# Halves and two PSUM banks at the start of a four-layer kernel, a bias transpose moved into K, a weight load moved ahead, and two layernorm statistics moved to ScalarE

## Chip, cores, metric

One core of one Trainium2 chip. The metric is the device time of one execution in microseconds (us), over several executions. Beside it stands the *span* in this text: the time from the first to the last of the program's own instructions in the profile, which every timed run reports too.

## The reference

```python
x = A_x                                             # (1, 2048, 1024) bf16
x = x + A(layernorm(x), wqkv, wo)                   # attention: 32 heads of 32, each position looks at
x = x + B(layernorm(x), w1, b1, w2, b2)             #   8 positions, 2 apart; B: 1024 -> 3584, gelu, -> 1024
x = x + A(layernorm(x), wqkv, wo)
x = x + B(layernorm(x), w1, b1, w2, b2)
```

## The kernel before

The 2048 rows are worked on in four groups of 512 rows (four tiles of 128). TensorE does Q, K, V, the output projection (with the weights Wq, Wk, Wv and Wo) and the two feed-forward products for one group after the other, in one fixed order. It puts its results into PSUM tiles, here one bank each, and VectorE or ScalarE copies them out. VectorE does the attention of one group while TensorE is at the products of another. The argument needs the start of the program and the first group's Q and K. `vec`, `act`, `pool` and `sp` are VectorE, ScalarE, GpSimd and the engine that issues most DMAs; with `.on` an engine keeps the order of the program text.

```python
load_x(0, 0, 2)                                     # x tiles 0 and 1
for k in range(0, KD, 2):                           # four pieces of Wq, 512 KB each, with x tiles 2 and 3 between
    load_wq_piece(...)
...
def ln_first():
    ...
    stats(0)                                        # VectorE: bn_stats x2, bn_aggr; ScalarE: sqrt
    stats(1)
    xn0 = norm(0)                                   # VectorE: reciprocal, (x - mean) * rstd
    xn1 = norm(1)
    transpose_on_pe(xn0, xa[0][:, 0, :, :], parts=[act.copy] * 4)      # 8 transposes into one PSUM bank, then copies
    ps = transpose_bias()                                              # b1, 28 x 128, on TensorE
    transpose_on_pe(xn1, xa[0][:, 1, :, :], parts=[vec.tensor_copy] * 2 + [act.copy] * 2)
    warm_up(2)                                                         # two matmuls of zeros
    act.copy(b1T[:], ps[:])
    stats(2); stats(3); ...
...
# first group: Q of tiles 0 and 1 as soon as they are there, then tiles 2 and 3, K, V
wk = load_qkv(1)
early_tiles = ln_early((1, None), (2, qk_next))     # groups 1 and 2: statistics and norm on VectorE, DMA transposes
...
# the main program
warm_up(14)
ln_first()
build_constants()
load_x(1)
load_x(2)                                           # third x group, ahead of Wk
stage(gen_qkv(0, qk_next=early), sides=at(14, load_b2))
```

## Time and profile before

| | kernel before |
|---|---|
| time, first three runs | 1230.68 us (1230.61 to 1230.74) |
| span of the profiled run | 1229.1 us |
| TensorE busy | 99% of the span |
| first useful matmul | 8.95 us |
| pitch of the 512-wide matmuls, 138 us to the end | 215.8 ns, no holes |

In the groups of instructions and in the timelines, a line has the start and the length in us, the engine, the source line (a helper's, as a rule), the operation, and out<-in by the program's names; brackets hold the idle time of the engine ahead of it and what ended it. PE is TensorE's matmuls, PEld its weight loads, SPq the queue that issues DMAs. The end of a matmul is modelled, so starts are what to reckon with. The lines that the argument rests on are in the prediction.

### The profile page before, as it was taken

The numbers are of one execution on the slowest core, as the hardware profiler recorded it, in microseconds if no ns is written. First come the engines' busy times: TensorE is split into PE (matmuls) and PEld (weight loads), VectorE is DVE, ScalarE is ACT, GpSimd is POOL, SyncE is SP. The second block draws the span as 40 slices with busy tenths as digits, with TensorE's granted clock in tenths as the row PEclk, the third lists the DMA queues.
The fourth block names the chain that finished last, engine by engine and source line by source line (L and its number), as shares of the span: only waits on it lengthen the run. The fifth ranks groups of instructions, "written<-read, shape, count | busy, mean of one in ns | idle before, by whom it ended". The sixth has DMA issues, their size and how long they took to land.

```text
span 1229.1 us, 13953 instructions
## 1 busy us (share of the span) xinstructions
PE 1221.3 (99%) x5723; PEld 632.7 (51%) x5773; DVE 864.2 (70%) x918; ACT 315.1 (26%) x507; POOL 105.2 (9%) x209
## 2 busy tenths in 40 slices
PE   9999999999999999999999999999999999999998
PEld 7666544456444564446544465444654444444444
DVE  8999896998997999375993759937599797011001
ACT  4343253014410144202441024410244001400310
POOL 3010015010101101100001000010000002000000
PEclk9999999999999999999999999999999999999999
DMA  9954674756648745856557565576664558446441
GB/s 299 293 205 154 178 238 153 201 171 206 215 133 239 188 151 167 235 169 181 155 160 233 171 171 175 155 222 202 171 199 145 189 195 203 155 160 195 154 136 52
DMA packets 220031, 226.64 MB, mean 184 GB/s; under 512 B 68194, under 2 KB 187136, under 8 KB 217920
## 3 DMA queue, kind: packets, MB, share of 16 engines
q1 hardware_dynamic: 214704, 208.69, 56.9%
q0 software_dynamic: 5264, 17.06, 3.6%
q8 instruction: 45, 0.74, 0.2%
q14 instruction: 18, 0.15, 0.0%
HBM read 189.01 MB, written 4.19 MB: 157 GB/s over the span
## 4 chain that ended last, share of the span: by engine, by line
PE 99%; DVE 0%; issue 0%; DMA 0%
PE acc L117 99%; DMA x<-in_A_x_dram 0%; DVE stats L92 0%; PE acc L218 0%; DVE xn L92 0%; DVE x L92 0%; DVE mv L92 0%; PE acc L181 0%; DVE rstd L92 0%
## 5 line engine op out<-in xcount | busy, mean ns | idle before, releaser
L117 PE MATMUL acc<-xnT,wt 128*128 128x512 bf16 (+1 forms) x3392 | 720.3, 375 | 0.1
L117 PEld LDWEIGHTS <-wt 128*128 128x128 bf16 x3392 | 400.8, 119 | 318.0 <-issue 0.5
L117 PE MATMUL acc<-wt,hT 128*128 128x512 bf16 (+1 forms) x1780 | 386.0, 376 | 2.1
L117 PEld LDWEIGHTS <-hT 128*128 128x128 bf16 x1820 | 178.1, 98 | 209.0
L92 DVE TENSOR_TENSOR big<-big 128x1024 bf16<-128x1024 bf16 (+2 forms) x184 | 244.7, 1358 | 2.2
L92 ACT ACTIVATE hT<-acc,b1T 128x512 bf16<-128x512 f32 x224 | 152.1, 687 | 325.1 <-PE acc L117 325.0
L92 DVE TENSOR_TENSOR big<-qT,kT 128x4096 bf16<-128x4096 bf16 x64 | 143.8, 2284 | 36.4 <-ACT kT L92 35.9
L92 DVE TENSOR_TENSOR tmp<-acc,b2bc 128x512 f32<-128x512 f32 x56 | 38.6, 689 | 161.6 <-PE acc L117 158.5
L92 DVE TENSOR_TENSOR big<-abc,vT 128x4096 bf16<-128x4096 bf16 x64 | 144.6, 2284 | 9.8 <-DMA abc<-a 7.4
L92 ACT CAST qT<-acc 128x512 bf16<-128x512 f32 (+1 forms) x72 | 38.2, 543 | 277.6 <-PE acc L117 277.6
L117 PE MATMUL acc<-wt,oT 128*128 128x512 bf16 x440 | 97.6, 379 | 0.5
L92 DVE BATCH_NORM_STATS2 stats<-x 128x6 f32<-128x512 bf16 x120 | 79.9, 680 | 3.7 <-DMA x<-in_A_x_dram 2.7
L117 PEld LDWEIGHTS <-oT 128*128 128x128 bf16 x448 | 43.8, 98 | 53.0 <-DVE oT L92 0.3
L92 DVE TENSOR_TENSOR x<-acc,big 128x512 bf16<-128x512 f32 (+1 forms) x9 | 5.7, 632 | 90.1 <-PE acc L117 90.0
L92 ACT CAST vT<-acc 128x512 bf16<-128x512 f32 x64 | 37.4, 585 | 100.9 <-PE acc L117 100.8
L92 POOL TENSOR_TENSOR rstd<-mv,eps_t 128x1 f32<-128x1 f32 x56 | 17.4, 311 | 527.5 <-DVE mv L92 527.5
L92 ACT CAST kT<-acc 128x512 bf16<-128x512 f32 x64 | 37.3, 585 | 68.7 <-PE acc L117 68.7
L92 DVE TENSOR_TENSOR x<-acc,x 128x512 bf16<-128x512 f32 x64 | 43.0, 672 | 4.9 <-PE acc L117 4.4
L92 DVE TENSOR_SCALAR xn<-x,mv,rstd 128x1024 bf16<-128x1024 bf16 x52 | 28.4, 546 | 19.9 <-POOL rstd L92 19.5
L92 DVE TENSOR_TENSOR x<-tmp,x 128x512 bf16<-128x512 f32 x56 | 38.6, 689 | 1.4
L92 POOL DMA_DIRECT2D big<-big x24 | 13.3, 563 | 212.8 <-DVE big L92 212.8
L92 POOL TENSOR_TENSOR rstd<-rstd,mhalf 128x1 f32<-128x1 f32 x56 | 30.9, 551 | 4.4
(63 smaller groups left out, 259.4 us busy)
## 6 DMA issues: line engine op xcount, KB each, us to landing
wt<-in_B_w_dram SPq DMA_DIRECT2D x56, 1024.0 KB, 5.8
wt<-in_B_w_dram SPq DMA_DIRECT2D x64, 896.0 KB, 4.9
wt<-in_A_wqkv_dram SPq DMA_DIRECT2D x46, 1024.0 KB, 5.7
wt<-in_A_wo_dram SPq DMA_DIRECT2D x16, 1024.0 KB, 5.3
abc<-a POOLq DMA_DIRECT2D x32, 256.0 KB, 4.7
big<-big POOLq DMA_DIRECT2D x24, 256.0 KB, 3.8
x<-in_A_x_dram SPq DMA_DIRECT2D x16, 256.0 KB, 5.7
out_dram<-x SPq DMA_DIRECT2D x31, 128.0 KB, 1.8
```

The source lines that it names most:

```text
L92: inst = f(*args, **kwargs)
L117: return pe(nc.tensor.matmul(*args, **kwargs))
```

## The change

Its intent: get TensorE to its first useful matmul earlier. Tile 1 is normalised and transposed in two halves, each in a bank of its own, so that VectorE and ScalarE can copy the halves out independently of each other. The bias transpose and two warm-up matmuls leave the start. Wk is loaded ahead of the third x group. Two tiles of that group get their statistics on ScalarE, and are normalised later, so that VectorE is free for the attention sooner. The core of the diff:

```diff
     def transpose_bias():
         ...
-        return ps
+        act.copy(b1T[:], ps[:])
...
-    def transpose_on_pe(xn, out, parts=None):
+    def transpose_on_pe(xn, out, parts=None, k0=0, k1=KD):
         pst = psum.tile([P, KD, P], BF16, name="acc", bufs=8)
-        for k in range(KD):
+        for k in range(k0, k1):
...
+        def norm(tt, parts=1):            # in ln_first: tensor_scalar on `parts` column ranges
...
-        xn1 = norm(1)
+        xn1 = norm(1, 2)
         transpose_on_pe(xn0, xa[0][:, 0, :, :], parts=[act.copy] * 4)
-        ps = transpose_bias()
-        transpose_on_pe(xn1, xa[0][:, 1, :, :], parts=[vec.tensor_copy] * 2 + [act.copy] * 2)
-        warm_up(2)
-        act.copy(b1T[:], ps[:])
+        transpose_on_pe(xn1, xa[0][:, 1, :, :], parts=[vec.tensor_copy] * 2, k1=KD // 2)
+        transpose_on_pe(xn1, xa[0][:, 1, :, :], parts=[act.copy] * 2, k0=KD // 2)
...
             wk = load_qkv(1)
         if n == 0:
+            load_x(2)
             early_tiles = ln_early((1, None), (2, qk_next))
...                                        # in ln_early: the last two tiles are left out ...
+        on_act = tiles[-2:]
+        tiles = tiles[:-2]
...
+    def ln_end():                          # ... normalised and transposed here, from ScalarE's statistics
+        for tt, (t, xn, xT) in zip((NTT - 2, NTT - 1), ln_rest.pop()):
+            ln_norm(t, mv_ahead[:, tt, :], rstd_ahead[:, tt, :], xn)
+            sp.dma_start_transpose(xT, xn.rearrange("s (k p) -> s k p", p=P))
...
         load_x(1)
-        load_x(2)
-        stage(gen_qkv(0, qk_next=early), sides=at(14, load_b2))
+        stage(gen_qkv(0, qk_next=early), sides=at(8, transpose_bias)
+              + at(9, ln_stats_ahead, 2, NTT - 2) + at(11, ln_end) + at(14, load_b2))
```

`at(8, f)` runs f's instructions after the ninth chunk of the first group, which is the first chunk of K.

## The prediction

> **What bounds the kernel now.** I read the head of the page first, then the chain of waits of the first 16 us, then the timeline of each engine there, and last the landings of the loads. The page says that TensorE is the bound almost everywhere:
>
> ```profile
> span 1229.1 us, 13953 instructions
> PE 1221.3 (99%) x5723; PEld 632.7 (51%) x5773; DVE 864.2 (70%) x918; ACT 315.1 (26%) x507; POOL 105.2 (9%) x209
> PE 99%; DVE 0%; issue 0%; DMA 0%
> ```
>
> The timeline of TensorE in the steady part shows whether those 99% are dense:
>
> ```profile
> 258.89 89.95 PE L117 MATMUL acc<-xnT,wt 128*128 128x512 bf16 x416
> 348.68 48.51 PE L117 MATMUL acc<-wt,hT 128*128 128x512 bf16 x219
> ```
>
> From the first start to the next group's start are 89.79 us for 416 matmuls, 215.8 ns each. The same pitch is found from 138 us to the end. Nothing in the change can shorten that, and it adds or removes no 512-wide matmul there. What can be won lies before the first useful matmul, and in the few short holes of the first 125 us. The chain of waits, first part:
>
> ```profile
> 6.58 0.56 DVE xn L92
> 7.14 0.05 issue
> 7.19 0.62 PE acc L218 x8
> 7.81 0.12 PE acc L181
> 7.92 0.55 PE acc L218 x8
> 8.48 0.43 PE acc L117 x2
> 8.91 0.04 issue
> 8.95 4.12 PE acc L117 x36
> ```
>
> The useful matmuls start at 8.95 us. Ahead of them stand eight transposes of tile 0 (L218), the bias transpose (L181), eight transposes of tile 1 and two warm-up matmuls. I don't believe the chain's last step. Two warm-ups that start at 8.31 take about 2 x 0.216 us of the array, so TensorE was free at 8.74. The timeline of VectorE names what it waited for:
>
> ```profile
> 7.24 0.55 DVE L92 TENSOR_SCALAR xn<-x,mv,rstd 128x1024 bf16<-128x1024 bf16 x1
> 8.52 0.49 DVE L92 COPY xnT<-acc 128x256 bf16<-128x256 bf16 x2 [0.73 <-PE acc L218]
> 8.92 1.27 DVE L92 BATCH_NORM_STATS2 stats<-x 128x6 f32<-128x512 bf16 x2
> ```
>
> The first of these two copies runs 8.52 to 8.81, and the first weight load of Wq is at 8.92. The instruction order of both kernels has that weight load wait on VectorE and on the first Wq piece, which landed at 6.75 (issued 1.65, 5.1 us to landing). So the chain that sets the start is: tile 1 normalised (7.79), all eight transposes into one bank (7.86 to 8.48), copy of its first quarter (8.81), 0.11 us to the weight load. The bias transpose is not on it: it runs while tile 1 is still being normalised. Nor are the warm-ups, which fill a wait.
>
> **What the Trainium skill says.** "TensorE: Matmul & The Clock Gate", section "Wait — 56ns, not 53.3ns?", gives N / 2.4 GHz plus about 2.5 ns: 215.7 ns at N = 512 and 55.6 at 128. The 215.8 ns above agree, and so do the transposes (eight starts in 0.45 us). "PSUM — Partial Sum Buffer", section "PSUM bank collisions raise a hardware error", says that two engines may not be in one bank (same 32 partitions) at once, so accesses to it are kept apart. In the trace ScalarE's fifth copy, the first out of tile 1's bank, starts only at 9.10, after VectorE's second copy out of the same bank ends at 9.00; the pitch of ScalarE's copies before is 0.26 us, so alone it would have started at 8.90. Two banks take that away, and let VectorE copy the first half while TensorE writes the second. "VectorE: DVE Perf Modes", section "The TRN2 errata — SBUF-src ops pay a fixed extra latency per instruction", warns that halving an operand doesn't halve the instruction; I take 0.31 us for half of the 0.548 us normalisation, an estimate. "DMA: Bandwidth & Descriptors", section "Queues, rings and completion order", says that each DMA engine takes descriptors in ring order. The trace agrees: x tile 4, issued at 5.16 us, lands at 12.86, after all the Wq pieces issued ahead of it. So whatever Wk gains by going ahead of the third x group, that group loses.
>
> **The change part by part.**
>
> (1) The start. Tile 0's transposes are unchanged: first at 7.19, ninth slot at 7.19 + 8 x 0.056 = 7.64. The first half of tile 1 is normalised at 7.24 + 0.31 = 7.55, plus 0.05 to TensorE, so its four transposes run without a wait from 7.64, with the last start at 7.81 and its end at 8.03 (0.22 each in the records). VectorE copies from 8.03 + 0.04 = 8.07 instead of 8.52. The second half is normalised by 7.82 and transposed by about 8.05, ahead of the first copy's end. First copy done 8.36, weight load 8.47, first matmul 8.50 instead of 8.95: -0.45 us. The two warm-ups (2 x 0.216 us) leave a hole that TensorE spends waiting; their removal gives nothing by itself, but left in they would have ended at about 8.5.
>
> (2) Whether this survives the next waits. Wq pieces 2, 3, 4 land at 8.97, 10.82 and 12.18 (issues plus 6.3, 7.2, 8.1 us). They are needed at 8.50 + 14 x 0.108 = 10.0, at 11.5 and at 13.5, so the least slack is 0.7 us. VectorE's statistics of tile 2 begin 0.46 earlier too, since they follow the copies; x tile 3 is there at 9.55, needed at 9.9. The late transposes keep their slack of 0.4 us. The gain stays.
>
> (3) The bias transpose goes into K, after its first chunk. One weight load and a 28-wide matmul between full matmuls: the next weight load can't be hidden behind so short a matmul. Its slot in the chain above is 0.12 us, and I take +0.08 us, an estimate. Its ScalarE copy (0.20 us) lies in idle time.
>
> (4) Wk ahead of the third x group. Wk's halves now land at 21.05 and 23.85 (issued 12.85 and about 13.5, 8.2 and 10.3 us to landing). Its second half is first needed at about 24.8: 0.9 us of slack, which the earlier start would cut to 0.45. Moved ahead, Wk lands about 1 MB / 390 GB/s = 2.7 us earlier. In this trace it held up nothing, so the gain is 0 here. The price: x tile 8 lands at about 21.9 instead of about 16.5, and VectorE, there at 19.8, waits some 2 us for it.
>
> (5) Two statistics to ScalarE. VectorE loses 2 x (1.28 + 0.21), with overlap about 2 x 1.36 = 2.7 us. It waits 2 us for tile 8, and its attention products start at about 27.0 instead of 28.60. Two normalisations of 0.5 us come later, between products, so VectorE is about 0.6 us ahead at 62 us. ScalarE gets four activations of 1.15 + 0.19 us (the durations of the same instructions later in the kernel) between K's casts, which have 1.14 us idle each. It delays casts by up to 2 us; eight accumulator banks are worth 8 x 1.73 us, so TensorE doesn't notice.
>
> (6) Where it could pay: the first output projection at 124 us, the only place where TensorE waits for something made on VectorE in this stretch. The timeline of the weight loads charges it to VectorE:
>
> ```profile
> 125.08 12.61 PEld L117 LDWEIGHTS <-oT 128*128 128x128 bf16 x59 [0.32 <-DVE oT L92]
> ```
>
> The hole in the cadence is really 125.08 - 124.66 - 0.216 = 0.2 us. It is at the fifth weight chunk, and the second half of Wo was issued at 119.87 and landed 5.1 us later, at 124.97. That load waits for a buffer that TensorE frees, so it moves with TensorE, and the hole stays. VectorE's last chunk (done 124.94) is not needed until 125.7.
>
> Sum: -0.45 + 0.08 = -0.37 us, so 1230.68 - 0.37 = 1230.3 us.
>
> **The rivals.** (a) The hole at 124 us is VectorE's after all, as that line has it. Then a VectorE that is ahead closes it: another -0.2, giving 1230.1. If VectorE is not ahead, because tile 8's wait and the later normalisations eat the saving, the 0.45 won at the start is waited out there, and the time is 1230.6 to 1230.7. Speaking for it: VectorE has no idle time from 28.6 to 124.9 but 2.0 us for a DMA, and its end at 124.94 fits as well as the landing at 124.97. Against it: the position in the chunk order. (b) The warm-ups matter for the clock, and TensorE falls back without them. The idle time is some 0.3 us after seven microseconds of work, and the hole of 1.1 us ahead of tile 0's transposes costs no clock now; I give it little. If it came, a few microseconds at half rate would cost 2 us or more: 1232 or more. (c) The late transposes of the third group by DMA (now behind Wk of the next stage in the same queue) hold up a later weight load. They are ready at about 43 us, take under 3 us each to issue (11.69 us for four now) and the load behind them can't be issued until V ends at 52 us. It lands some 5 us after its issue, at 57, and is needed after four chunks of Q (4 x 1.73) and half a chunk of K, at about 59.5. So a slip of 2 us beyond 52 is free, and one of 3 would cost 0.5 us or so, 1230.8. I expect none.
>
> **Range and chances.** Steps (1) and (3) are each uncertain by 0.1 us, rival (a) by -0.2 to +0.4, and the runs before spread over 0.13 us. I put 1229.7 to 1230.75 for 8 in 10. Two per cent would be 24.6 us; the whole time before the first useful matmul is 9 us, so faster by that is impossible without something unseen, and slower needs a stall that repeats over the eight groups, which no moved instruction touches.
>
> **What would show it.** Right: the first Wq matmul at about 8.5 us; VectorE's first copy at about 8.07; the first K cast 0.4 us earlier, the second by 0.08 less; VectorE waiting about 2 us on x tile 8 at 20 us; four 1.15 us activations on ScalarE between K's casts; the hole of 0.2 us at 124 us unchanged; every later group's start earlier by the same 0.4 us. Wrong: a first matmul near 8.9 (something other than the copy held it), a hole in K, a hole at 124 us that grew or vanished, or a matmul pitch above 0.108 us at 9 us.

## The result

The changed kernel takes 1231.06 us (median of 6 runs, 1230.80 to 1231.31), the kernel before 1230.71 (6 runs, 1230.61 to 1231.29). The ratio is 1.0002, with a 95% interval of 0.9989 to 1.0015: the class "same", as predicted, but outside the predicted range of 1229.7 to 1230.75. (Ratios here are the mean time of one kernel's fast runs over that of the other's of the same rounds, so not quite the ratio of the medians.) All runs told here gave the right result.

The puzzle is in the first line of the page of the changed kernel:

```profile
span 1228.7 us, 14007 instructions
PE 1223.1 (100%) x5771; PEld 632.5 (51%) x5771; DVE 862.1 (70%) x913; ACT 319.2 (26%) x515; POOL 108.7 (9%) x211
```

The span is 0.36 us *shorter* than before (1228.72 against 1229.07 in the traces; the first expectation below rounds it to 0.37), the predicted sum but for 0.01, while the time is 0.35 us *longer*. In the timed runs the changed kernel's time is 2.10 to 2.19 us above its span; in the one run of the kernel before that had both numbers then, it was 1.74 (1230.84 and 1229.1).

The chain of waits of the changed kernel, to be read against the eight lines of it in the prediction:

```profile
7.12 0.93 PE acc L220 x12
8.06 0.02 issue
8.08 0.30 DVE xnT L92
8.38 0.14 issue
8.52 4.13 PE acc L117 x36
...
15.29 10.03 PE acc L117 x84
25.32 0.12 PE acc L181
25.44 1200.27 PE acc L117 x5588
```

Twelve transposes, not sixteen, now precede the copy; the copy itself is on the chain, as the prediction had read it; the first Wq matmul is at 8.52. The bias transpose (L181) stands in K. After it, the chain is TensorE to the end. TensorE's weight loads around it:

```profile
23.87 1.01 PEld L117 LDWEIGHTS <-wt 128*128 128x128 bf16 x5
25.25 0.09 PEld L181 LDWEIGHTS <-abc 28*128 28x128 bf16 x1 [0.38 <-issue]
25.37 1.07 PEld L117 LDWEIGHTS <-wt 128*128 128x128 bf16 x6
```

Within K a weight load follows 0.216 us after the one before. The bias's load starts 0.38 us after the end of the last: it was not pulled ahead of the running matmul, and TensorE stood for 0.1 us. That is more than the prediction had for the whole.

VectorE's wait for x tile 8 came as worked out (2 us at 20 us forecast, with products from 27.0):

```profile
22.17 1.29 DVE L92 BATCH_NORM_STATS2 stats<-x 128x6 f32<-128x512 bf16 x2 [1.86 <-DMA x<-in_A_x_dram]
```

Its products start at 27.14 instead of 28.60. The hole at the first output projection is gone in this trace: that group of 64 matmuls takes 13.98 us, as all later ones do, against 14.17 before. So far the span and the start say "right", but two of the prediction's own signs of being wrong are there as well: a hole in K (at the bias), and a hole at 124 us that vanished. The experiments had to find why the clock says otherwise.

### The profile page after: what moved, and what is told of

Same layout as the page of the kernel before. It is cut to its first block, busy times and chain, and to the rows that moved or that the text cites. A ratio compares the mean times of both kernels' runs of the same rounds, so it can differ in the third digit from the quotient of the medians.

```text
span 1228.7 us, 14007 instructions
## 1 busy us (share of the span) xinstructions
PE 1223.1 (100%) x5771; PEld 632.5 (51%) x5771; DVE 862.1 (70%) x913; ACT 319.2 (26%) x515; POOL 108.7 (9%) x211
## 4 chain that ended last, share of the span: by engine, by line
PE 99%; DVE 0%; DMA 0%; issue 0%
PE acc L117 99%; DMA x<-in_A_x_dram 0%; DVE stats L92 0%; PE acc L220 0%; DVE xn L92 0%; DVE x L92 0%; DVE mv L92 0%; DVE xnT L92 0%; PE acc L181 0%; DVE rstd L92 0%
## 5 line engine op out<-in xcount | busy, mean ns | idle before, releaser
L92 DVE TENSOR_SCALAR xn<-x,mv,rstd 128x1024 bf16<-128x1024 bf16 (+1 forms) x53 | 28.6, 542 | 20.1 <-POOL rstd L92 19.7
```

The source lines that it names most:

```text
L92: inst = f(*args, **kwargs)
```

## The experiments

Eighteen runs, in five jobs; the runs of one job share their runs of the kernel before. Three kinds of numbers are read from each: the time, the span of each run, and the one trace that each label leaves.

### 1. Both kernels once more, and each half of the change

**before_again** and **after_again**: the two kernels, no edit.

> The kernel before, unchanged, for the one number that the record of its timed runs lacks: the span of each run beside its time. Fact to explain: in the two traces the changed kernel's span is 0.37 us shorter (1228.7 against 1229.1), as the prediction's sum said, yet its time is 0.35 us longer (1231.06 against 1230.71). In the changed kernel's runs time minus span is 2.1 us; in the one run of before that has both it is 1.7. Theory A (what lies outside the program's own instructions belongs to the built program): time minus span is 1.6 to 1.75 us in all runs here, spans 1229.0 to 1229.1. Theory B (it drifts from job to job or chip to chip, and the changed kernel met a bad one): time minus span scatters between 1.6 and 2.2 here. Theory C (the profiled runs of the changed kernel are at the lucky end of a span that scatters, the timed ones are longer): spans scatter here over 0.5 us too.

> The changed kernel, unchanged. Theory A: time minus span 2.1 us again in every run, spans 1228.7 to 1229.2, time 1230.8 to 1231.3. Theory B: in one job with the kernel before, both have the same time minus span, and the changed kernel is 0.3 to 0.4 us faster.

**start_only**: the new start, with the bias transpose in TensorE's hole; the rest as before.

```diff
# against the changed kernel
+        transpose_bias()                   # at the end of tile 1's transposes
-        ... at(8, transpose_bias) + at(9, ln_stats_ahead, 2, NTT - 2) + at(11, ln_end) +
-            load_x(2)                      # back ahead of Wk; the last two tiles back in ln_early
```

> The start of the changed kernel alone (halves, two banks, no two warm-ups), with the bias transpose put into the hole that TensorE has between the last transpose of tile 1 and the first Wq matmul; Wk's place and all statistics as before. Prediction's steps: first Wq matmul at 8.5 us, span 1229.1 - 0.45 = 1228.65. Rival (a) of the prediction, that VectorE then holds the first output projection: the hole at 124 us grows from 0.2 to about 0.6 us and the span is back at 1229.1. Theory A says nothing of the time minus span beforehand; if it is 1.7 here, the extra 0.4 us come with Wk's move or the statistics, if 2.1 with the new start.

**rest_only**: Wk's move and ScalarE's statistics, with the old start.

```diff
# against the changed kernel
-        xn1 = norm(1, 2)  ... two banks
+        xn1 = norm(1)     ... one bank, transpose_bias() ahead of it, warm_up(2) after it
-        ... at(8, transpose_bias) +
```

> The rest alone: the start as before, Wk ahead of the third x group, two statistics on ScalarE. Prediction's steps (4) and (5): worth nothing by themselves, span 1229.1. Rival (a): the hole of 0.2 us at 124 us closes since VectorE is ahead, span 1228.9. Time minus span 1.7 or 2.1 shows whether the extra 0.4 us come with this part.

Measured, five runs each:

| | median time | spans of the runs | time minus span |
|---|---|---|---|
| before, shared (9 runs) | 1231.39 | 1228.8 to 1230.5 | 1.73 to 1.84 |
| before_again | 1230.96 | 1228.9 to 1229.8 | 1.75 to 1.82 |
| after_again | 1231.25 | 1228.6 to 1229.6 | 2.08 to 2.15 |
| start_only | 1231.25 | 1229.0 to 1231.5 | 1.85 to 1.92 |
| rest_only | 1230.76 | 1228.6 to 1229.4 | 1.82 to 1.87, once 2.01 |

Theory B (a bad job) falls: in one job, on one chip, the changed kernel has 0.3 us more outside its span than the kernel before, in each of its runs. Theory A stands. Theory C is right as well: the spans of one and the same kernel scatter over 1.7 us, over four times what the change was to win, so two single traces agreeing with a sum to 0.01 us was luck. The ratios (1.0000 for after_again, 1.0003 and 0.9997 for the halves) tell nothing apart.

Where the scatter comes from shows in the traces. The first Wq piece is issued at 1.65 us in all twenty traces, and lands anywhere from 6.15 to 8.40; all later loads follow it in order. The trace of before has it at 6.71, that of start_only at 8.40. TensorE's timeline in start_only:

```profile
8.45 1.75 PE L117 MATMUL acc<-xnT,wt 128*128 128x256 bf16 x14
10.62 1.75 PE L117 MATMUL acc<-xnT,wt 128*128 128x256 bf16 x14 [0.43 <-DMA wt<-in_A_wqkv_dram]
12.57 1.09 PE L117 MATMUL acc<-xnT,wt 128*128 128x256 bf16 x8 [0.20 <-DMA wt<-in_A_wqkv_dram]
...
26.37 27.87 PE L117 MATMUL acc<-xnT,wt 128*128 128x512 bf16 x128 [0.89 <-DMA wt<-in_A_wqkv_dram]
54.76 5.40 PE L117 MATMUL acc<-xnT,wt 128*128 128x512 bf16 x24 [0.52 <-DMA wt<-in_A_wqkv_dram]
```

The first matmul is early (8.45), and then TensorE waits for the second and third piece of Wq (landed 10.58 and 12.53), for Wk's second half (26.33), and for the next group's Wq (54.72), which stands in the queue behind four DMA transposes. What was won at the start is lost to loads. So slack of under 1 us against a landing, as the prediction had it for Wq, Wk and Wo, is no slack here.

The rival of the hole at 124 us is decided too. In both traces of the changed kernel VectorE ends its part equally early (124.49 and 124.48). But the second half of Wo, issued at 119.72 and 119.74, lands at 124.66 in the first and at 125.53 in the second, and in the second TensorE waits again:

```profile
123.86 1.03 PE L117 MATMUL acc<-wt,oT 128*128 128x512 bf16 x3
125.57 13.11 PE L117 MATMUL acc<-wt,oT 128*128 128x512 bf16 x59 [0.68 <-DMA wt<-in_A_wo_dram]
```

It is the load, as the prediction said against the profile's own label. It neither "stays at 0.2" nor goes away by the change: it is 0 to 0.84 us, by the landing.

### 2. Taking one part out, and a placebo

**bias_in_hole**: the changed kernel with the bias transpose where TensorE waits anyway.

```diff
         transpose_on_pe(xn1, xa[0][:, 1, :, :], parts=[act.copy] * 2, k0=KD // 2)
+        transpose_bias()
...
-        sides=at(8, transpose_bias) + at(9, ln_stats_ahead, 2, NTT - 2) + ...
+        sides=at(9, ln_stats_ahead, 2, NTT - 2) + ...
```

> The changed kernel with the bias transpose taken out of K and put into the hole after tile 1's transposes. The last runs showed the bias in K to cost 0.15 us (holes of 0.096 and 0.055 us around it), so the least span should fall from the changed kernel's 1228.6 to 1228.45. Time minus span, so far 1.78 in the kernel before, 1.88 in each half of the change and 2.11 in the whole: theory A (fixed by the built program, not by a part of the change) leaves open what comes, anything from 1.7 to 2.2, but the same in all five runs within 0.08; a theory that K's bias transpose is what it comes from (the one thing in the whole that neither half had) says 1.8 to 1.9 here.

**no_wk_move**: the changed kernel with `load_x(2)` back ahead of Wk.

> The changed kernel without Wk's move (new start, bias in K, statistics on ScalarE). Late state of the loads (first Wq piece at 8.2 us or later): Wk's second half lands at 25 to 26 and is needed at 24.4, a hole of about 1 us at K, as in the run of the start alone. Early state (6.7 us): Wk lands at 23.9, no hole. So least span as the changed kernel's, 1228.6, but a longer tail: the highest of the five 1 us or more above it. If the prediction's step (4), that the move gains nothing, holds in every state, the spread is that of the changed kernel.

**no_act_stats**: the changed kernel with all statistics on VectorE (the two `on_act` lines and the two sides taken out).

> The changed kernel with all statistics on VectorE as before (new start, bias in K, Wk moved). x tiles 8 to 11 now land at 22 to 24 us, and VectorE takes their statistics after that, so it ends its part about 4 us later than with two of them on ScalarE, some 2 to 3 us later than in the kernel before. Prediction's step (6), that the last output chunk has 0.75 us of slack at 124 us, then says a hole of about 2 us there: span about 1230.5 to 1231. If VectorE did not matter at all, span 1228.6 to 1229.

**placebo**: the kernel before and two instructions that do nothing.

```diff
         pool.memset(mask[:], 0.0)
+        pool.memset(mask[:], 0.0)
+        pool.memset(mask[:], 0.0)
```

> The kernel before with two more memsets of the mask on GpSimd at 3 us, which nothing waits for: spans must be those of the kernel before (1228.8 to 1230.5, by the state of the loads). It is there for the time minus span. Theory A in its plainest form (any other program shifts it by some tenths, for no reason in the change): something other than 1.78, the same in all runs. If it stays 1.78 within 0.03, the extra time belongs to what the change does.

| | median time | spans of the runs | time minus span |
|---|---|---|---|
| before, shared (9 runs) | 1230.82 | 1228.6 to 1229.8 | 1.75 to 1.83 |
| bias_in_hole | 1230.95 | 1228.4 to 1229.6 | 2.07 to 2.16 |
| no_wk_move | 1230.97 | 1228.8 to 1229.3 | 2.10 to 2.17 |
| no_act_stats | 1231.38 | 1228.7 to 1230.8 | 1.82 to 1.88 |
| placebo | 1231.15 | 1228.6 to 1230.2 | 1.73 to 1.82 |

**The bias.** The least span is 0.2 us below the changed kernel's. The traces give the cost without any scatter: from the first Wq matmul to the first weight load of the first output projection are 115.115 us in the changed kernel and in no_wk_move, and 114.847 to 114.851 in bias_in_hole, placebo, before and pad_dve (below), none of which has a hole there. So 28 columns transposed between full matmuls cost 0.27 us (my 0.15 in the expectation counted only two of the three gaps). In the hole it costs nothing:

```profile
7.50 1.24 PE L220 MATMUL acc<-ident,xn 128*128 128x128 bf16 x16 [1.75 <-DVE xn L92]
8.67 0.18 PE L181 MATMUL acc<-ident,abc 28*128 28x28 bf16 x1
8.89 0.63 PE L117 MATMUL acc<-xnT,wt 128*128 128x256 bf16 x4
```

Here x tile 0 landed late (3.88), which is why all starts are later than in the changed kernel's trace; from that landing to the first Wq matmul are 5.01 us in both.

**Wk's move.** The expected tail did not show in no_wk_move's five runs, and its one trace had the loads in between (first Wq piece 7.23, Wk 23.90, no hole at K). That test is inconclusive. What the traces do show: with Wk in its old place its second half landed at 23.74 to 26.33, and TensorE waited for it twice in five traces (0.16 and 1.05 us); ahead of the third x group it landed at 21.2 to 23.4, and TensorE waited in none of fifteen.

**ScalarE's statistics.** The expectation for no_act_stats, a hole of about 2 us at 124, was a miss: no such hole. VectorE did start its products late (29.13 against 27.14), but ended only 1.3 us later (125.80 against 124.49), since its one DMA wait at 90 us shrank from 2.06 to 0.53 us, and TensorE had more to wait for elsewhere (0.61 us for Wq in all, counted from matmul start to matmul start; none in the changed kernel's trace). Its median span is still the highest of the job.

**Time minus span.** The placebo left it alone, and so did the removal of the bias from K. The programs with 2.1 have the new start *and* the statistics on ScalarE; those with one of the two have 1.8 to 1.9 (one run of rest_only has 2.01).

### 3. Is the extra time an accident of layout?

All four on bias_in_hole, each with a few instructions more on one engine, at a time when it idles.

```diff
# pad_pool
+        pool.memset(mask[:], 0.0)   # twice
# pad_dve
+    for _ in range(6):
+        vec.memset(spare[:], 0.0)
# pad_act
+    for _ in range(7):
+        act.activation(one[:], eps_t[:], ACT.Sqrt)
# pad_pe
-    warm_up(14)
+    warm_up(15)
```

> The kernel of the run with the bias in the hole (time minus span 2.12, and 2.12 also in both other kernels that have the new start and the ScalarE statistics together; 1.78 to 1.86 in the six that have not both) with two more memsets of the mask on GpSimd at 3 us, which nothing waits for. Theory A1 (the extra 0.33 us is an accident of how the built program lies, and comes and goes with a few instructions on some engine): about 1.8 here or in one of the other three. Theory A2 (it is a cost of what the change does): 2.12 in all four. Spans 1228.4 to 1229.6 in both.

> The same kernel with six memsets of an unused tile on VectorE at 1 us, where it idles until 3.5. A1: time minus span about 1.8 here or in one of its three neighbours. A2: 2.12. Spans 1228.4 to 1229.6.

> The same kernel with seven more one-column activations on ScalarE at 2 us (about 1.4 us, done before it is wanted at 5.1). The instructions that both the three slow kernels have more of are ScalarE's (eight for the statistics). A1: time minus span about 1.8 here or in one of its three neighbours. A2: 2.12. Spans 1228.4 to 1229.6.

> The same kernel with 15 first warm-up matmuls instead of 14 (done at 5.9 to 7.4 us). The new start took three pairs of instructions from TensorE; this gives one back. A1: time minus span about 1.8 here or in one of its three neighbours. A2: 2.12. Spans 1228.4 to 1229.6, perhaps 0.1 to 0.2 more where the warm-ups run cold and end after tile 0 is normalised at 7.1.

Time minus span was 2.09 to 2.20 in all twenty runs (medians 2.12, 2.17, 2.11, 2.12), against 1.72 to 1.84 in the nine shared runs of before. Padding on GpSimd, ScalarE and TensorE doesn't move it, so for these three theory A1 falls. For VectorE it stays open. The view of the DMA queues in pad_dve's trace from 1229 to 1231 us, when the span is over (1228.46), has one line:

```profile
q14 instruction: 1, 0.01, 1.4%
```

It is an 8 KB fetch of instructions, from 1.60 to 2.04 us after the span's end; the other nineteen traces have none that ends after the span. The last semaphore record of pad_dve's trace comes 2.27 us after the span's end, those of the other nineteen at 1.90 to 1.99. So pad_dve's 2.17 may be the extra of its neighbours or a new one in its place. Spans: 1228.4 to 1229.6, as expected.

pad_pe's trace shows one more thing, which the prediction had as rival (c) and gave nothing:

```profile
38.73 20.94 PE L117 MATMUL acc<-xnT,wt 128*128 128x512 bf16 x96 [0.41 <-DMA wt<-in_A_wqkv_dram]
59.97 2.38 PE L117 MATMUL acc<-xnT,wt 128*128 128x512 bf16 x10 [0.30 <-DMA wt<-in_A_wqkv_dram]
```

The first wait is for Wv, which landed late like the loads before it (38.68). The second is for the next group's Wk, whose issue stands behind the two moved DMA transposes. The queue's own timeline in that run:

```profile
40.67 1.65 SPq L92 DMA_DIRECT2D wt<-in_A_wqkv_dram  x3
44.57 9.69 SPq L92 DMA_TRANSPOSE xnT<-qT  x2
54.36 1.08 SPq L92 DMA_DIRECT2D wt<-in_A_wqkv_dram  x2
```

They take the queue 9.69 us, not two times 3, and the load goes out at 54.36 instead of at 52 or before. The hole is 0.47 us at 59.97, about what the prediction said such a slip would cost. This is no matter of one run: in all twelve traces with two tiles put off, the two transposes take 7.87 to 9.89 us, and the load goes out at 51.57 to 54.37, against 50.59 to 51.43 in the three of the kernel before and the placebo. TensorE waited for it in two of the twelve (0.14 us in rest_no_warm, below).

### 4. Which part of each half does it take?

**rest_banks**: rest_only with `norm(1, 2)` and the two banks; bias and warm-ups where they were. **rest_no_warm**: rest_only without `warm_up(2)`.

> The statistics and Wk's move, with tile 1 in halves and two banks, but with the bias transpose and the two warm-ups where they were. Time minus span is 2.12 if the halves and banks are what it takes beside the statistics, 1.86 if it is the removed warm-ups or the bias. Spans: the warm-ups end at about 8.55, so the first Wq matmul at 8.7 to 8.8, 5.2 to 5.3 us after x tile 0's landing instead of 5.38 before and 5.01 in the changed kernel.

> The statistics and Wk's move, with the old start but for the two warm-ups, which are left out. Prediction's step (1): they only fill a wait, so the first Wq matmul stays at 5.38 us after x tile 0's landing. Time minus span 2.12 if the warm-ups' removal is what it takes beside the statistics, else 1.86.

**idle_stats**: no_act_stats, with ScalarE's statistics made as well and not used.

```diff
-        sides=at(8, transpose_bias) + at(14, load_b2)
+        sides=at(8, transpose_bias) + at(9, ln_stats_ahead, 2, NTT - 2) + at(14, load_b2)
```

> The new start and Wk's move, VectorE with all its own statistics as in the kernel before, and the two tiles' statistics on ScalarE and GpSimd as well, with a result that nothing uses. Time minus span 2.12 if ScalarE's work is what it takes beside the new start; 1.83 if it is what is taken from VectorE and put later (the two normalisations and transposes).

**one_act_tile**: bias_in_hole with the statistics of one tile on ScalarE instead of two.

```diff
-        on_act = tiles[-2:]
-        tiles = tiles[:-2]
+        on_act = tiles[-1:]
+        tiles = tiles[:-1]
...
-        for tt, (t, xn, xT) in zip((NTT - 2, NTT - 1), ln_rest.pop()):
+        for tt, (t, xn, xT) in zip((NTT - 1,), ln_rest.pop()):
...
-        at(9, ln_stats_ahead, 2, NTT - 2)
+        at(9, ln_stats_ahead, 2, NTT - 1)
```

> The kernel with the bias in the hole, with one tile's statistics on ScalarE instead of two. Time minus span 2.12 if the cost is a switch, about 2.0 if it grows with the number of tiles. Spans 1228.4 to 1229.5; VectorE about 1.3 us later at 62 us than with two tiles.

| | median time | spans of the runs | time minus span |
|---|---|---|---|
| before, shared (7 runs) | 1231.15 | 1228.8 to 1229.7 | 1.74 to 1.83 |
| rest_banks | 1230.87 | 1228.4 to 1229.1 | 2.10 to 2.14 |
| rest_no_warm | 1231.21 | 1228.9 to 1229.5 | 1.78 to 1.82, once 2.04 |
| idle_stats | 1231.82 | 1229.8 to 1230.4 | 1.84 to 1.91 |
| one_act_tile | 1230.67 | 1228.3 to 1229.3 | 1.77 to 1.82 |

Of the start it takes the halves and banks (rest_banks against rest_only). Of the statistics, ScalarE's work alone is not enough (idle_stats); two tiles have to be taken off VectorE and made good later, and one doesn't do it. No run takes them off VectorE without giving them to ScalarE. So it looks like a switch rather than a cost that grows, but not a clean one: start_only and idle_stats lie about 0.1 us above the kernel before, and of the nine runs of rest_only and rest_no_warm one each has 2.01 and 2.04.

One rival was not separated from this. The pages' counts of VectorE's instructions sort the programs just as well: 913 in every program with 2.12 but pad_dve, 912 in rest_only and rest_no_warm, 916 with one tile, 918 and 919 in the others. The halves are one more VectorE instruction, and each tile put off is three fewer. So what matters may be the length of VectorE's program and not what the change does in it; pad_dve, with 919, is the only run that could tell, and its late fetch spoils it.

The start itself, in the same unit as above: from x tile 0's landing to the first Wq matmul are 5.38 us in before, before_again, rest_only and rest_no_warm, 5.01 in all programs with the whole new start, and 5.17 in rest_banks, where the two warm-ups are still in front. So the removal of the warm-ups is worth nothing with the old start (rest_no_warm), as predicted, and 0.16 us with the new one: left in they are the bound, where the prediction had them end at about 8.5, just in time. (placebo's trace has 5.53. There x tile 0 had landed unusually early, at 3.19, and the last of the first 14 warm-up matmuls started only at 6.50: tile 0's transposes began 0.18 us after the tile was normalised, 0.06 in all other traces.)

idle_stats is the one program in which VectorE did hold the output projection. With all statistics its own and x tiles 8 to 11 loaded behind Wk, it ends at 126.39 (no_act_stats, which has this in common, at 125.80, and there TensorE doesn't wait), and its trace has the wait that rival (a) described:

```profile
124.21 0.96 PEld L117 LDWEIGHTS <-oT 128*128 128x128 bf16 x5
125.50 0.10 PEld L117 LDWEIGHTS <-oT 128*128 128x128 bf16 x1 [0.32 <-DVE big L92]
126.11 0.10 PEld L117 LDWEIGHTS <-oT 128*128 128x128 bf16 x1 [0.52 <-DVE oT L92]
126.45 11.98 PEld L117 LDWEIGHTS <-oT 128*128 128x128 bf16 x57 [0.24 <-DVE oT L92]
```

This is how a wait on VectorE looks: it is at the seventh and eighth weight load (oT's last two chunks), not at the sixth, where Wo's second half is waited for.

### 5. The best version and the changed kernel once more

> The same kernel as one_act_tile once more, with more rounds, as the candidate for the fastest version: time minus span 1.77 in all runs, spans 1228.3 to 1229.3, so 0.4 us faster than the kernel before in the same job in the median, which is still less than the scatter of one kernel's runs and inside the 2% class. If the first result was luck of the loads, the medians are equal within 0.1 us.

> The changed kernel in the same job: time minus span 2.11 again, median about 0.1 us slower than the kernel before and 0.5 slower than one_act_again.

one_act_again: 1230.61 us median, spans 1228.6 to 1229.7, time minus span 1.73 to 1.82. after_third: 1231.09, spans 1228.7 to 1229.3, time minus span 2.08 to 2.14. The shared runs of before: 1230.86. So one_act_again is 0.25 us faster than before, not 0.4, and the changed kernel 0.23 slower, not 0.1. All runs that report a span, taken together:

| | runs | mean time | mean span | least span | time minus span, mean |
|---|---|---|---|---|---|
| kernel before | 48 | 1230.98 | 1229.20 | 1228.6 | 1.78 |
| changed kernel | 16 | 1231.13 | 1229.01 | 1228.6 | 2.12 |
| one tile on ScalarE, bias in the hole | 9 | 1230.68 | 1228.90 | 1228.3 | 1.78 |

So the last version is the fastest seen, by 0.3 us against the kernel before; its ratios to before (0.9998 in both jobs, intervals of 0.0012 and more on both sides) don't make that certain. Its chain after the start is TensorE without a break from 15.42 us on:

```profile
15.42 1210.15 PE acc L117 x5672
```

## Why the prediction was wrong

**The step that failed is the last one of its sum**: "1230.68 - 0.37 = 1230.3 us", the time taken to change by what the span changes by, with a range built on the 0.13 us of three runs. Two things fell through it. The first is the 0.34 us that the changed kernel takes outside the span of its own instructions (2.12 against 1.78, in 16 and 48 runs, without overlap). No view of a profile of before could show it. In the programs that were run it comes with tile 1's halves and banks together with two tiles put off on VectorE, and padding on three other engines doesn't move it. Whether it is these or the length of VectorE's program, and what it *is*, stays open: no instruction of the program is recorded there, and the last semaphore record after the span's end is at 1.90 us in the first traces of both kernels. The second is the scatter of the span, 1228.6 to 1230.5 for one unchanged kernel, which three lucky runs had hidden: the mean time of all 48 is 1230.98, 0.3 us above them.

**Step (1), the start: right in mechanism, mis-sized.** VectorE's copy did hold the first matmul, and the bank's wait for eight transposes did hold the copy. Gained: 5.38 - 5.01 = 0.37 us, not 0.45. The term that was off is the half normalisation, taken as 0.31 us:

```profile
L92 DVE TENSOR_SCALAR xn<-x,mv,rstd 128x512 bf16<-128x512 bf16 x2 | 0.7, 410 | 0.0
```

It took 0.41, so that tile 1's first transpose had to wait a little, and the chain ended 0.08 us later.

**Step (3), the bias in K: mis-sized by three times.** 0.27 us, not 0.08. The prediction saw that the next weight load can't be hidden; it missed that the bias's own weight load isn't either. Steps (1) and (3) together make -0.37 + 0.27 = -0.10 us; the mean spans differ by -0.19. The -0.36 of the first two traces has two more parts, both luck of the loads: x tile 0 landed 0.06 us earlier (3.51 against 3.57), and the hole of 0.20 us at 124 us was missing.

**Step (2), "the gain stays": too strong.** With the first Wq piece 1.3 to 1.7 us later than in the trace that was read (no_act_stats, pad_pool, start_only), the earlier start ends in waits for Wq. Where it landed at 8.2 with the old start (before_again) and the new one (pad_pool), TensorE waits 0.30 and 0.74 us for Wq: the difference, 0.44, is all that the start had won and a little more. The slacks of 0.7 us were read off one execution.

**Step (4), Wk: right for that execution only.** When the loads are late, Wk in its old place holds K by up to 1 us; in its new place it never did. The price, VectorE's 2 us for x tile 8, was right (1.86), though one reading was not: in the kernel before the tile lands at 15.55, not at about 16.5. Nothing hangs on that.

**Steps (5) and (6): right.** Products at 27.14 (27.0 forecast); 0.62 us ahead at 62 us (0.6 forecast: 61.95 against 62.58); casts delayed without effect on TensorE; the hole at 124 us belongs to Wo's load (it landed at 125.03; the prediction's landing times, sums of rounded numbers, are up to 0.06 us off). Rival (a) can happen, and did in idle_stats, not in the changed kernel. Rival (b), a clock that falls back, didn't: the 36 matmuls at 8.5 us take 4.13 us, as before. Rival (c), of which the prediction expected nothing, happens when the loads are late: the two transposes take some 9 us to issue, not under 3 each.

Added up: -0.37 + 0.27 + 0.34 = +0.24 us forecast with the right sizes; measured +0.35 in the medians of the first job and +0.15 in the means of all runs.

## What to carry to other kernels

Before predicting tenths of a microsecond, ask for the scatter of the unchanged kernel's span over many runs, and for the time outside the span: here both are as large as what the change wins, and a second trace of the kernel before would have shown that slacks against landings vary by 1.5 us. A small transpose belongs where TensorE waits anyway, not between full matmuls. And a part that is worth nothing in one trace can still keep TensorE from waiting in another (Wk's move when the loads are late; in idle_stats, statistics left on VectorE held TensorE up); judge it in the execution with the late loads.

## What the Trainium skill lacked or had wrong

- "TensorE: Matmul & The Clock Gate", section "Step-by-step: what each phase is for", says that TensorE pulls weight loads ahead of running matmuls when the row groups don't conflict or the load goes to the background weight buffer. For a 28-column transpose put between 512-wide matmuls it did not: the transpose's weight load began 0.38 us after the one before had ended, and the transpose cost 0.27 us in all. Which condition was not met, no run shows, and the page has no figure for such an interruption.
- "VectorE: DVE Perf Modes", section "The TRN2 errata — SBUF-src ops pay a fixed extra latency per instruction", puts the measured fixed term at about 150 cycles, for a copy. For a bf16 tensor_scalar with two per-partition scalars, 1024 columns took 0.548 us and 512 took 0.410: by that difference a fixed part of 0.27 us, an estimate, some 260 cycles at the page's 0.96 GHz. (The same 1024 columns written to another tile took 0.49 us, so one fixed part doesn't fit all.)
- "DMA: Bandwidth & Descriptors", section "Latency and other measured facts", has figures for first bytes and for HBM access. It says nothing of how much the same load varies from one execution to the next: a 512 KB load, issued at 1.65 us of every execution behind two of 256 KB, landed between 6.15 and 8.40 us in twenty traces.
- No page says that a kernel's time and the span of its instructions can part by different amounts in two versions of one kernel: 1.78 and 2.12 us here, steady to within 0.08 us in each.
